# Probabilities times v in 64x64 quadrants, two units a visit, in a fused attention and feed-forward kernel

## The chip, the cores and the metric

The kernel runs on one core of a Trainium2 chip, in one launch. The metric is the device time of a run in microseconds (us), from the first to the last instruction with what lies around them. Times of the kernel before: 998.48, 1001.32 and 998.5 us, median 998.5. The engines are named as in the profile: PE does matrix products (PEld is its weight load, which overlaps them), DVE and ACT work on whole tiles and are the two that this kernel lets read PE's results, POOL scales tiles, and SP issues transfers.

## The reference, cut to what matters

Causal attention with a window of 128 positions and a slope per head, then a two-layer network on its output:

```
batch, heads, seq, dim = 8, 8, 576, 64
scores = q @ k.T / 8 + slope[h] * -(i - j)      where 0 <= i - j < 128, else -1e9
attn   = softmax(scores)
x      = (attn @ v), heads side by side         -> 4608 x 512
h      = x @ w_in                               512 x 2048
g      = h * erf(softplus(h))
out    = g @ w_out                              2048 x 512
```

All of it is float32.

## The kernel before

**Units.** The 4608 rows are cut into 12 chunks of 384. A unit is one chunk for two heads, so there are 48 units, four to a chunk, and `u // 4` is the chunk. Two chunks of three (32 units) are the first and second row blocks of a batch entry; every third chunk (`last`, 16 units) gathers the last 192 rows of two entries. `Attention.unit` plans one unit: it loads q, k and v (`load`), makes the scores of both heads in 64x64 tiles of PE (`scores`, line 478), adds the bias on DVE (505), exponentiates on ACT (515), sums and inverts on DVE (528, 529), scales on POOL (538), transposes on PE (557) into PSUM tiles `t`, copies those into `pT` (DVE or ACT, 417 and 415), and multiplies `pT` by v on PE (590) into a PSUM tile `px`. `px` is then copied as the high part of x (417 or 415) and subtracted from (600) to give the low part: fp32 numbers are split in two so that the network's products run in three quick passes.

**v times probabilities.** Here v lies in memory as 128 rows (64 positions of head 0, 64 of head 1) by 128 columns, in which head 0's rows hold zeros in head 1's columns and the other way round. One product of a 64-position block thus does both heads at once with a 128x128 weight, half of it zeros. A unit has six such products (four 192 columns wide, one 128, one 64), a unit of the last kind ten (two of 192, four of 128, four of 64). Each product is two records in the profile.

**Three stages.** Attention and the network's first pass run together: 6 of the 16 slices of the network's inner dimension, for each chunk as soon as its x is there (`h` line 797, `o` line 860). Meanwhile DVE and ACT bring the weights into two parts and park them in memory (lines 632 to 691). When all attention and all weight work is done, its memory is given back (`close`), the parked weights are fetched (720), and the second pass does the other ten slices (lines 999 and 1070).

**What sets the order.** `Plan.run` is a list scheduler that runs before the kernel is built. Every operation has a cost by engine, a due time `at` and the buffers that it takes; the plan goes through time, gives each engine the ready operation of lowest `at`, and writes each engine's instructions in that order, for good. Where an operation may go to DVE or ACT, the plan chooses. Buffers come from rings: PSUM tiles `s`, `t` and `px` share one ring `a` of three banks, v's ring has `NQ` buffers, `pT`'s has `TB`.

Of the kernel before, what the change touches and what calls it, by code (L numbers as in the profile page):

```python
# [8 lines left out]
F32 = mybir.dt.float32  # L9
# [8 lines left out]
B, H, S, D = 8, 8, 576, 64  # L18
NPAIR = H // 2
P = 128  # L20
# [3 lines left out]
NK = DM // P  # L24
NF = FF // P
CH = 384
# [11 lines left out]
WARM = 30  # L38

MB, KH, KS = 17, 3, 3  # L40
NQ, NKB, PB, XB, OB, TB = 2, 4, 9, 5, 5, 2

TE, NE = 4, 6
TA = 6.5
LL, LN, LT = 26, 0, 0
SQ = 0.36
LEAD = 45

# [10 lines left out]
TS, VL, NQF, SLP = 9, 8, 4, True  # L59
WB, PIE = "o1", 2  # L60
VE = -17
# [7 lines left out]
SUB = ALU.subtract  # L69
# [268 lines left out]
def fp32_us(n):  # L338
    return 2 * max(n / 1200.0 + 0.003, 0.111)


def dve(n, fast=False):
    return 0.047 + n * (0.00054 if fast else 0.00108)


def act(n, aps=0, src=0.088):
    return src + 0.093 * aps + n * 0.00084


def dma(nbytes, n=1, run=1536, eng="SP", out=False):  # L350
    packet = 9 + 0.0367 * run
    return dict(costs={eng: n * 0.42}, moved=nbytes / run * packet / 16e3 + 0.05 * n * (run > 2048), packet=packet, after=0.9 if out else 1.8 if run > 2048 else 1.3, count=n)


def unit_time(u):
    return TE * min(u, NE) + TA * max(0, u - NE) + UNITS.get(u, 0)
# [13 lines left out]
class Attention:  # L370


    def __init__(self, tc, plan, ctx, actx, qk, v, bias, ident, moe):
        self.nc, self.plan = tc.nc, plan
        self.qk, self.v = qk, v
        self.ident, self.moe = ident, moe
        nc, op = self.nc, plan.op
        sb = lambda name: actx.enter_context(tc.tile_pool(name=name, bufs=1))
        biases = sb("biases")
        self.bias = []  # L380
        rel = Buf(shape=[P, 4, D], ap=biases.tile([P, 4, D], F32, name="rel"))
        op(emit=lambda e: nc.scalar.dma_start(rel.all, bias), w=[rel], at=-40, **dma(P * 4 * D * 4, run=1024, eng="Act"))
        for g in range(NPAIR):
            b = Buf(shape=[P, 2, 4, D], ap=biases.tile([P, 2, 4, D], F32, name=f"bias{g}"))

            def slopes(e, b=b, g=g):
                for j in range(2):
                    slope = 2.0 ** (2 - 2 * g - j)
                    if e == "Act":
                        nc.scalar.mul(b[:, j], rel.all, slope)  # L390
                    else:
                        nc.gpsimd.tensor_scalar(b[:, j], rel.all, slope, 1.0, op0=ALU.mult, op1=ALU.mult)

            op({"Pool": 2 * (0.24 + 4 * D * 0.00086)} if SLP and g else {"Act": 2 * act(4 * D)}, slopes, r=[rel], w=[b], at=unit_time(g) - LL + 6)
            self.bias.append(b)
        self.ps_of = {}
        self.kp, self.pp, self.ptp, self.vp = (sb(n) for n in ("kp", "pp", "ptp", "vp"))
        self.ps = ctx.enter_context(tc.tile_pool(name="ps_a", bufs=1, space=PSUM))
        self.warm_up()
        for u in range(4 * moe.nch):  # L400
            self.unit(u)

    def warm_up(self):

# [14 lines left out]
    def load(self, u):  # L419


        c, g = u // 4, u % 4
        nc, op = self.nc, self.plan.op
        at = unit_time(u) - LL
        last = c % 3 == 2
        n, m = (640, 10) if last else (448, 6)
        i = c // 3 if last else c - c // 3
        src, vsrc = self.qk[last][i, g], self.v[last][i, g]
        qk = Buf(self.kp, [P, CH + 640], F32, "qk", NKB, f"qk{u}")
        v = Buf(self.vp, [P, 10, 2, D], F32, "v", NQ, f"v{u}")  # L430
        rows = lambda j: slice(j * D, (j + 1) * D)
        q = lambda t, j, h: qk[rows(j), t * P + h * D : t * P + (h + 1) * D]
        k = lambda j, x, w: qk[rows(j), CH + x : CH + x + w]
        if u:
            parts = [[qk]] * 3
            op(emit=lambda e: nc.sync.dma_start(qk[:, : CH + n], src), w=[qk], at=u - 29 if u < NQF else at, **dma(P * (CH + n) * 4, run=(CH + n) * 4))
        else:
            pieces = [Part(qk, i) for i in range((4, 2, 1)[PIE])]
            for i, (eng, issue, lo, hi) in enumerate(((
                    ("SP", nc.sync, 0, P), ("Act", nc.scalar, CH, CH + 192), ("Act", nc.scalar, CH + 192, CH + n), ("SP", nc.sync, P, CH)),  # L440
                    (("SP", nc.sync, 0, CH), ("SP", nc.sync, CH, CH + n)), (("SP", nc.sync, 0, CH + n),))[PIE]):
                op(emit=lambda e, issue=issue, lo=lo, hi=hi: issue.dma_start(qk[:, lo:hi], src[:, lo:hi]), w=[pieces[i]], at=-40 + i,
                   **dma(P * (hi - lo) * 4, run=(hi - lo) * 4, eng=eng))
            parts = [pieces[:2], pieces, pieces]
        op(emit=lambda e: nc.sync.dma_start(v[:, :m].rearrange("p x j d -> p (x j d)"), vsrc), w=[v], at=VE + 2 * u if u < NQF else at + VL,
           **dma(P * m * 2 * D * 4, run=m * 2 * D * 4))
        return parts, q, k, v

    def scores(self, u, ts, q, k, loaded, early, pts):
# [32 lines left out]
    def unit(self, u):  # L482


        nc, op = self.nc, self.plan.op
# [54 lines left out]

                op({"Pool": 2 * (0.24 + (3 - c0) * D * 0.00086)}, scaled, r=[p[t], sums[t]], w=[p[t]], at=at)

        at += LT
        px_at = at
        pT = Buf(self.ptp, [P, 8 * 192], F32, "pT", TB, f"pT{u}")
        run = lambda x, n, w: pT[:, x : x + n * w].rearrange("p (l c) -> p l c", c=w)
        parts = []
        for t in range(3):
            c0 = 0 if last or t else 1
# [11 lines left out]

            op({"PE": 0.109 * (3 - c0) + 0.005}, transposes, r=[p[t]], w=[ps], at=at)
            w = (3 - c0) * D
            step, x = (192, t * 384) if not last else ((192, 0), (192, 576), (576, 384))[t]
            part = Part(pT, slice(None), t)
            parts.append(part)

            def out(e, ps=ps, w=w, step=step, x=x):
                two = ps[:, : 2 * 192].rearrange("p (l c) -> p l c", c=192)
                self.copy(e, run(x, 2, step)[:, :, :w], two[:, :, :w])  # L570

            op({"DVE": dve(2 * w), "Act": act(2 * w, src=0.053)}, out, r=[ps], w=[part], at=at)

        px = Buf(self.ps, [P, 512], F32, "a", 3, f"px{u}", keep=0)
        if last:
            todo = [[(3 * s, kk, 5 * s + kk) for s in range(2) for kk in (2, 0, 1, 3, 4)]]
        else:
            todo = [[(0, 2, 0)], [(x, 2, x) for x in (3, 1, 2, 4, 5)]]
        for n, group in enumerate(todo):
            terms = []  # L580
            for base, kk, blk in group:
                if last:
                    i0, i1 = max(0, kk - 2), min(2, kk)
                    terms.append((blk, (base + i0) * 192 + (2 - kk + i0) * D, i1 - i0 + 1, (base + i0) * D))
                else:
                    terms.append((blk, base * 192, min(3, 6 - base), base * D))

            def products(e, terms=terms, first=n == 0, end=n + 1 == len(todo)):
                for x, (blk, src, m, to) in enumerate(terms):
                    nc.tensor.matmul(  # L590
                        px[:, to : to + m * D], lhsT=v[:, blk].rearrange("p j d -> p (j d)"), rhs=run(src, m, 256)[:, :, :D],
                        start=first and x == 0, stop=end and x + 1 == len(terms))

            op({"PE": sum(fp32_us(m * D) for _, _, m, _ in terms) + 0.005}, products,
               r=[v, *(parts if n or last else parts[:2])], w=[px], at=at + 0.1)

        hi, lo = self.moe.x_parts[c][g]
        op({"DVE": dve(CH), "Act": act(CH, src=0.053)},
           lambda e: self.copy(e, hi.all, px[:, :CH]), r=[px], w=[hi], at=at + 0.1)
        op({"DVE": dve(CH)}, lambda e: nc.vector.tensor_tensor(lo.all, px[:, :CH], hi.all, SUB),  # L600
           r=[px, hi], w=[lo], at=at + 0.1)
        if g % 2:
            self.moe.save_x(c, g // 2, at + 0.1)


class Weights:
# [560 lines left out]
def _layout(q, k, v, moe_w_in, moe_w_out):  # L1167
# [7 lines left out]
    qk_a = flat(np.concatenate([qT[..., :CH], gap, kT[..., :CH]], 4))  # L1175
    both = lambda a, lo, hi: [a[s::2, ..., lo:hi] for s in range(2)]
    qk_c = flat(np.concatenate([*both(qT, CH, 512), *both(qT, 512, S), *both(kT, 256, S)], 4))
    vs = np.zeros((nb, NPAIR, 2, D, S // D, 2, D), np.float32)
    for b in range(nb):
        for j in range(2):  # L1180
            vs[b, :, j, :, :, j] = v[b, j::2].reshape(NPAIR, S // D, D, D).transpose(0, 2, 1, 3)
    v_a = np.ascontiguousarray(vs[..., :6, :, :]).reshape(nb, NPAIR, P, 768)
    v_c = np.concatenate([vs[s::2, ..., 4:, :, :].reshape(nb // 2, NPAIR, P, 640) for s in range(2)], 3)
    bits = lambda a: a.view(np.int64)
    wi = np.ascontiguousarray(bits(moe_w_in).reshape(NK, P, NF, P).transpose(2, 1, 0, 3))
    wo = np.ascontiguousarray(bits(moe_w_out))
    row = (np.arange(P) % 64)[:, None]
    rel = WIN + row - np.arange(192)[None, :]
# [25 lines left out]
```

## Time and profile before

| what | value |
|---|---|
| runs | 998.48, 1001.32, 998.5 us |
| span of the profiled execution | 996.5 us |
| median less span | 2.0 us |
| busy in the span | PE 983.5, PEld 873.2, DVE 682.7, ACT 668.9, POOL 155.0 us |
| DMA | 172.17 MB, mean 173 GB/s |

The page gives the span of one profiled execution; the 2.0 us by which the median is above it are what lies before the first and after the last instruction. A line such as L590 is line 590 of the kernel. PE's busy time counts a matmul from its start to its modelled end; since matmuls overlap, the durations of single records sum to more than the time that a group takes. What a group takes is read in the chain of waits, whose pieces do not overlap.

### The profile page before, as it was taken

The page shows a single profiled execution, that of the slowest core. Times are in us where ns is not written, and L with a number is a line of the kernel's source. Part 1 is how long each engine was busy: PE and PEld are TensorE (multiplying, and loading weights), DVE is VectorE, ACT ScalarE, POOL GpSimd, SP SyncE. Part 2 cuts the span into 40 slices and gives each one's busy share as a digit, 9 for nine tenths or more (in the row PEclk, how much of TensorE's full clock was granted, in tenths as well). Part 3 has the DMA queues.
Part 4 walks back from the last instruction along what each step waited for, and adds up shares of the span by engine and source line. Part 5 has one row for each costly group of instructions (what it writes and reads, how often), then busy time and mean ns, then how long its engine had stood idle before and what let it go on. Part 6 is the DMA issues. An engine that isn't in the chain of part 4 may idle for free.

```text
span 996.5 us, 17094 instructions
## 1 busy us (share of the span) xinstructions
PE 983.5 (99%) x6168; PEld 873.2 (88%) x6168; DVE 682.7 (69%) x1627; ACT 668.9 (67%) x1261; POOL 155.0 (16%) x300
## 2 busy tenths in 40 slices
PE   9899999999999999999999999999999999999998
PEld 7788898888888888889999899898998989989896
DVE  6999899789998987465557367367457547544433
ACT  6898788888878878667866464545555464464652
POOL 4613433223314432131000000000000000000000
PEclk9999999999999999999999999999999999999999
DMA  9754685678875675554974243152242341420302
GB/s 366 268 168 146 223 269 172 255 269 300 283 265 174 236 258 183 175 191 156 373 259 148 86 183 116 44 190 75 85 161 80 109 159 43 147 96 2 125 1 74
DMA packets 63076, 172.17 MB, mean 173 GB/s; under 512 B 7056, under 2 KB 7184, under 8 KB 62992
## 3 DMA queue, kind: packets, MB, share of 16 engines
q1 hardware_dynamic: 62848, 170.95, 49.5%
q8 instruction: 49, 0.80, 0.4%
q14 instruction: 35, 0.29, 0.1%
q10 hardware_dynamic: 144, 0.13, 0.0%
HBM read 118.88 MB, written 52.17 MB: 172 GB/s over the span
## 4 chain that ended last, share of the span: by engine, by line
PE 89%; DVE 7%; ACT 2%; issue 1%; POOL 1%; DMA 1%; SPq 0%; DVEq 0%; POOLq 0%
PE o L860 14%; PE h L797 13%; PE pa L999 13%; PE po L1070 12%; PE pa L1070 12%; PE px L590 8%; PE pc L999 6%; PE s L478 4%; PE t L557 4%; PE pb L999 3%; DVE p L505 1%; ACT p L515 1%; POOL p L538 1%; PE warm_ps L410 1%; DVE wti L637 0%
## 5 line engine op out<-in xcount | busy, mean ns | idle before, releaser
L538 POOL TENSOR_SCALAR p<-p,st 128x192 f32<-128x192 f32 (+1 forms) x288 | 152.0, 550 | 293.1 <-DVE st L529 175.6
L797 PE MATMUL h<-x,wi 128*128 128x384 f32 x864 | 174.3, 344 | 0.0
L780 ACT COPY hs<-pa 128x384 f32<-128x384 f32 x92 | 44.3, 481 | 180.1 <-PE pa L999 179.5
L797 PEld LDWEIGHTS h<-x,wi 128*128 128x128 f32 x864 | 149.2, 188 | 7.9 <-issue 4.2
L860 PE MATMUL o<-wo,gh 128*128 128x512 f32 x432 | 141.6, 408 | 0.0
L515 ACT ACTIVATE p<-p,st 128x192 f32<-128x192 f32 (+1 forms) x288 | 123.9, 433 | 16.3 <-DVE st L505 16.2
L999 PE MATMUL pa<-t,p 128*128 128x384 f32 x540 | 108.9, 336 | 0.0
L590 PEld LDWEIGHTS px<-pT,v 128*128 128x128 f32 x704 | 100.7, 191 | 5.8 <-DVE x L600 2.0
L590 PE MATMUL px<-pT,v 128*128 128x192 f32 (+2 forms) x704 | 102.4, 296 | 1.7 <-DVE x L600 1.7
L999 PEld LDWEIGHTS pa<-t,p 128*128 128x128 f32 x540 | 96.4, 188 | 5.9
L1070 PE MATMUL po<-ho,gh 128*128 128x512 f32 x270 | 91.0, 391 | 0.0
L1070 PE MATMUL pa<-ho,gh 128*128 128x512 f32 x270 | 90.5, 389 | 0.0
L782 DVE COPY hs<-pa 128x384 f32<-128x384 f32 x28 | 15.6, 557 | 108.4 <-PE pa L999 108.4
L860 PEld LDWEIGHTS o<-wo,gh 128*128 128x128 f32 x432 | 75.1, 189 | 13.6 <-issue 4.7
L860 PE MATMUL o<-wo,gl 128*128 128x512 f32 x216 | 85.3, 395 | 0.0
L505 DVE CUSTOM_DVE_ANT_0 p<-s,bias 128x192 f32<-128x192 f32 x224 | 66.2, 350 | 8.0 <-PE s L478 7.7
L1070 PE MATMUL po<-ho,gl 128*128 128x512 f32 x180 | 71.3, 396 | 0.0
L1050 DVE TENSOR_TENSOR hs<-s,hs 128x768 f32<-128x768 f32 x60 | 56.2, 951 | 20.9 <-ACT s L1042 20.9
L1070 PE MATMUL pa<-ho,gl 128*128 128x512 f32 x180 | 70.1, 389 | 0.0
L1010 DVE TENSOR_TENSOR hs<-pc,hs 128x384 f32<-128x384 f32 x60 | 33.3, 556 | 52.0 <-PE pc L999 37.7
L557 PE MATMUL t<-ident,p 128*128 128x128 f32 x400 | 62.1, 275 | 4.0 <-POOL p L538 2.5
L557 PEld LDWEIGHTS t<-ident,p 128*128 128x128 f32 x400 | 48.0, 143 | 15.2 <-POOL p L538 6.8
(259 smaller groups left out, 1858.8 us busy)
## 6 DMA issues: line engine op xcount, KB each, us to landing
xd<-x SPq DMA_DIRECT2D x24, 768.0 KB, 6.0
qk<-qk_a SPq DMA_DIRECT2D x32, 416.0 KB, 4.8
v<-v_a SPq DMA_DIRECT2D x32, 384.0 KB, 3.8
v<-v_c SPq DMA_DIRECT2D x16, 640.0 KB, 4.1
pd<-ot SPq DMA_DIRECT2D x36, 256.0 KB, 3.3
out<-pd SPq DMA_DIRECT2D x36, 256.0 KB, 4.0
p<-wd SPq DMA_DIRECT2D x35, 256.0 KB, 5.3
wri<-w_in SPq DMA_DIRECT2D x16, 512.0 KB, 7.2
```

Source lines behind the costliest of these rows:

```text
L478: nc.tensor.matmul(bank[h * D : (h + 1) * D, x : x + n], lhsT=q(t, j, h), rhs=k(j, off[h], n), start=True, stop=True)
L505: nc.vector.tensor_tensor_reduce(out=pt[:, c0:, j, :], in0=ps[j][0][:, ps[j][1] : ps[j][1] + n].rearrange("p (c d) -> p c d", d=D), in1=se ...
L515: nc.scalar.activation(dst, dst, AF.Exp, bias=low[t][:, j : j + 1], scale=-1.0, accum_out=sums[t][:, j : j + 1])
L538: nc.gpsimd.tensor_scalar(dst, dst, sums[t][:, j : j + 1], 1.0, op0=ALU.mult, op1=ALU.mult)
L557: nc.tensor.matmul(two[:, :, (2 - cb) * D : (3 - cb) * D], lhsT=p[t][:, cb].rearrange("p j d -> p (j d)"), rhs=self.ident[:, :], is_transp ...
L590: nc.tensor.matmul(px[:, to : to + m * D], lhsT=v[:, blk].rearrange("p j d -> p (j d)"), rhs=run(src, m, 256)[:, :, :D], start=first and x ...
L780: self.nc.scalar.copy(out, src)
L797: nc.tensor.matmul(ps[:, :CH], lhsT=ww[:, cs], rhs=xx[:, k], start=(k2 + k + n == 0), stop=(k2 + k + n == 4),)
L860: nc.tensor.matmul(po.all, lhsT=g[:, j, cs], rhs=w.all, start=(u["start"] and n == 0), stop=(u["end"] and n == 2),)
L999: nc.tensor.matmul(dst[:, :CH], lhsT=wv[i](k), rhs=xb[l][:, k], start=start and k + n == 0, stop=k + n == 3, skip_group_check=not start)
L1050: op({"DVE": dve(2 * CH)}, lambda e, s=s, hs=hs: V.tensor_tensor(hs.all, s.all, hs.all, ALU.mult), r=[s, *parts], w=parts, at=at, port=True)
L1070: nc.tensor.matmul(po.all, lhsT=g[:, k, cs], rhs=w.all, start=start and n == 0, stop=end and n == 2)
```

## The change

Scores are already made in 64x64 tiles; now v times probabilities is too. v comes without zeros (`v` is 128 rows by 64 columns a block, half the bytes), and the two units of a pair are multiplied in one visit of PE (`pair`), after both are transposed. A block's four products are head 0 and 1 of the first unit and head 1 and 0 of the second, one for each quadrant of the array: rows by the head, since that is where v and `pT` lie, columns by the head for the first unit and swapped for the second. Products from the upper 64 rows all go to PSUM bank `px[0]`, those from the lower ones to `px[1]`. So `px[0]` holds heads 0 and 2 of the four, `px[1]` heads 3 and 1, and the rows of w_in are put into that order before the launch. `pT` keeps its data in another layout (18 blocks of 64), its ring has 3 buffers in place of 2, v's has 4 in place of 2. Copies and subtractions of `px` are as many and as large as before.

```diff
--- before.py
+++ after.py
-NQ, NKB, PB, XB, OB, TB = 2, 4, 9, 5, 5, 2
+NQ, NKB, PB, XB, OB, TB = 4, 4, 9, 5, 5, 3
...
-LL, LN, LT = 26, 0, 0
+LL, LN, LT, PXL = 26, 0, 0, 0.1
...
-        for u in range(4 * moe.nch):
-            self.unit(u)
+        for u in range(0, 4 * moe.nch, 2):
+            self.pair(u, [self.unit(u), self.unit(u + 1)])
...
-        v = Buf(self.vp, [P, 10, 2, D], F32, "v", NQ, f"v{u}")
+        v = Buf(self.vp, [P, 10, D], F32, "v", NQ, f"v{u}")
...
-        pT = Buf(self.ptp, [P, 8 * 192], F32, "pT", TB, f"pT{u}")
-        run = lambda x, n, w: pT[:, x : x + n * w].rearrange("p (l c) -> p l c", c=w)
+        pT = Buf(self.ptp, [P, 18, D], F32, "pT", TB, f"pT{u}")
...
-            step, x = (192, t * 384) if not last else ((192, 0), (192, 576), (576, 384))[t]
+            ys = slice(2 * t, 2 * t + 2) if not last else (slice(0, 2), slice(3, 5), slice(2, 6, 3))[t]
...
-                self.copy(e, run(x, 2, step)[:, :, :w], two[:, :, :w])
+                every = pT[:, :].rearrange("p (y b) d -> p y (b d)", b=3)
+                self.copy(e, every[:, ys, :w], two[:, :, :w])
...
-        px = Buf(self.ps, [P, 512], F32, "a", 3, f"px{u}", keep=0)
-        if last:
...
-            def products(e, terms=terms, first=n == 0, end=n + 1 == len(todo)):
-                for x, (blk, src, m, to) in enumerate(terms):
-                    nc.tensor.matmul(
-                        px[:, to : to + m * D], lhsT=v[:, blk].rearrange("p j d -> p (j d)"), rhs=run(src, m, 256)[:, :, :D],
-                        start=first and x == 0, stop=end and x + 1 == len(terms))
-
-            op({"PE": sum(fp32_us(m * D) for _, _, m, _ in terms) + 0.005}, products,
-               r=[v, *(parts if n or last else parts[:2])], w=[px], at=at + 0.1)
...
+        return v, pT, parts
+
+    def pair(self, u, units):
+
+        nc, op = self.nc, self.plan.op
+        c, g = u // 4, u % 4
+        last = c % 3 == 2
+        at = unit_time(u + 1) + LN + LT + PXL
+        px = [Buf(self.ps, [P, 512], F32, "a", 3, f"px{u + j}", keep=0) for j in range(2)]
+        terms = []
+        for s, kk in [(s, kk) for s in range(2) for kk in (2, 0, 1, 3, 4)] if last else [(0, kk) for kk in (0, 3, 1, 2, 4, 5)]:
+            if last:
+                i0, i1 = max(0, kk - 2), min(2, kk)
+                first = 3 * s + i0
+                terms.append((5 * s + kk, 3 * first + 2 - kk + i0, i1 - i0 + 1, first * D))
+            else:
+                terms.append((kk, 3 * kk, min(3, 6 - kk), kk * D))
+
+        def products(e):
+            for x, (blk, src, m, to) in enumerate(terms):
+                for swap, (v, pT, _) in enumerate(units):
+                    for j in (swap, 1 - swap):
+                        rows, cols = slice(j * D, (j + 1) * D), slice((j ^ swap) * D, ((j ^ swap) + 1) * D)
+                        nc.tensor.matmul(
+                            px[j][cols, to : to + m * D], lhsT=v[rows, blk, :], rhs=pT[rows, src : src + 4 * m - 3 : 4, :],
+                            start=x == 0, stop=x + 1 == len(terms))
+
+        op({"PE": SQ + sum(2 * max(m * D / 1200 + 0.002, 0.06) for _, _, m, _ in terms)}, products,
+           r=[b for v, _, parts in units for b in (v, *parts)], w=px, at=at)
+        for j in range(2):
+            hi, lo = self.moe.x_parts[c][g + j]
+            op({"DVE": dve(CH), "Act": act(CH, src=0.053)},
+               lambda e, hi=hi, j=j: self.copy(e, hi.all, px[j][:, :CH]), r=[px[j]], w=[hi], at=at)
+            op({"DVE": dve(CH)}, lambda e, hi=hi, lo=lo, j=j: nc.vector.tensor_tensor(lo.all, px[j][:, :CH], hi.all, SUB),
+               r=[px[j], hi], w=[lo], at=at)
+        self.moe.save_x(c, g // 2, at)
...
-    vs = np.zeros((nb, NPAIR, 2, D, S // D, 2, D), np.float32)
-    for b in range(nb):
-        for j in range(2):
-            vs[b, :, j, :, :, j] = v[b, j::2].reshape(NPAIR, S // D, D, D).transpose(0, 2, 1, 3)
-    v_a = np.ascontiguousarray(vs[..., :6, :, :]).reshape(nb, NPAIR, P, 768)
-    v_c = np.concatenate([vs[s::2, ..., 4:, :, :].reshape(nb // 2, NPAIR, P, 640) for s in range(2)], 3)
+    vs = np.ascontiguousarray(v.reshape(nb, NPAIR, 2, S // D, D, D).transpose(0, 1, 2, 4, 3, 5)).reshape(nb, NPAIR, P, S // D, D)
+    v_a = np.ascontiguousarray(vs[..., :6, :]).reshape(nb, NPAIR, P, 384)
+    v_c = np.concatenate([vs[s::2, ..., 4:, :].reshape(nb // 2, NPAIR, P, 320) for s in range(2)], 3)
     bits = lambda a: a.view(np.int64)
-    wi = np.ascontiguousarray(bits(moe_w_in).reshape(NK, P, NF, P).transpose(2, 1, 0, 3))
+    heads = [h + 4 * k2 for k2 in range(NPAIR // 2) for h in (0, 2, 3, 1)]
+    wi = bits(moe_w_in).reshape(H, D, NF, P)[heads].reshape(NK, P, NF, P)
+    wi = np.ascontiguousarray(wi.transpose(2, 1, 0, 3))
```

The order of instructions moves with it. In PE's order, the visits of units 26 and 27 stood like this before (px is the product, t a transpose, o and h products of the first pass; a number behind a name is that of the unit or slice):

```order
L590 MATMUL px26_3391<-pT26_3330,v26_3140 128x192 x4
L590 MATMUL px26_3391<-pT26_3330,v26_3140 128x128
L590 MATMUL px26_3391<-pT26_3330,v26_3140 128x64
L557 MATMUL t27_0_3404<-ident_62,p27_0_3280 128x2x64 x2
L557 MATMUL t27_1_3409<-ident_62,p27_1_3284 128x2x64 x3
L860 MATMUL o0_24_3415<-wo0_1033,gh24_2956 128x512 x2
L860 MATMUL o0_24_3415<-wo0_1033,gl24_2975 128x512
L860 MATMUL o1_24_3425<-wo0_1033,gh24_2956 128x512 x2
L860 MATMUL o1_24_3425<-wo0_1033,gl24_2975 128x512
L557 MATMUL t27_2_3435<-ident_62,p27_2_3294 128x2x64 x3
L590 MATMUL px27_3441<-pT27_3419,v27_3202 128x192
```

and stand like this now, as the first ten of 24 rows of one visit (line 590 is now 595, 557 is 554):

```order
L864 MATMUL o1_24_3578<-wo0_1123,gh24_3206 128x512 x2
L864 MATMUL o1_24_3578<-wo0_1123,gl24_3210 128x512
L595 MATMUL px26_3585<-pT26_3461,v26_3218 64x192
L595 MATMUL px27_3587<-pT26_3461,v26_3218 64x192
L595 MATMUL px27_3587<-pT27_3525,v27_3225 64x192
L595 MATMUL px26_3585<-pT27_3525,v27_3225 64x192
L595 MATMUL px26_3585<-pT26_3461,v26_3218 64x192
L595 MATMUL px27_3587<-pT26_3461,v26_3218 64x192
L595 MATMUL px27_3587<-pT27_3525,v27_3225 64x192
L595 MATMUL px26_3585<-pT27_3525,v27_3225 64x192
```

Unit 26's products stood alone ahead of unit 27's transposes; now all of the pair's stand in one run behind the transposes of both.

At the end of attention on PE, unit 47's product and what follows it, before:

```order
L797 MATMUL h59_5824<-x9_0_4647,wi5_959 128x384 x6
L797 MATMUL h59_5824<-x9_1_4984,wi5_959 128x384 x6
L590 MATMUL px47_5845<-pT47_5803,v47_5684 128x192
L590 MATMUL px47_5845<-pT47_5803,v47_5684 128x64
L590 MATMUL px47_5845<-pT47_5803,v47_5684 128x128 x2
L590 MATMUL px47_5845<-pT47_5803,v47_5684 128x64
L590 MATMUL px47_5845<-pT47_5803,v47_5684 128x192
L590 MATMUL px47_5845<-pT47_5803,v47_5684 128x64
L590 MATMUL px47_5845<-pT47_5803,v47_5684 128x128 x2
L590 MATMUL px47_5845<-pT47_5803,v47_5684 128x64
L860 MATMUL o0_48_5455<-wo5_1448,gh52_5491 128x512 x2
L860 MATMUL o0_48_5455<-wo5_1448,gl52_5513 128x512
```

and now, the end of the visit of units 46 and 47:

```order
L595 MATMUL px46_6091<-pT46_6008,v46_5665 64x64
L595 MATMUL px47_6093<-pT46_6008,v46_5665 64x64
L595 MATMUL px47_6093<-pT47_6071,v47_5669 64x64
L595 MATMUL px46_6091<-pT47_6071,v47_5669 64x64
L801 MATMUL h57_6081<-x9_1_5240,wi3_900 128x384 x6
L864 MATMUL o0_48_5812<-wo3_1423,gh50_5724 128x512 x2
L864 MATMUL o0_48_5812<-wo3_1423,gl50_5757 128x512
L864 MATMUL o0_48_5812<-wo4_1542,gh52_5869 128x512 x2
L864 MATMUL o0_48_5812<-wo4_1542,gl52_5914 128x512
```

The visit now stands ahead of the second half of slice-unit h57 and of h58 and h59, which were done by then before. Counted to the end of the first pass, 144 h and 171 o products stood behind the last px, now 174 and 189.

On DVE, the end of the last weight's preparation (wto15) stood beside the copies of unit 40's transposes before:

```order
L640 SCALAR_TENSOR_TENSOR wqo15_4801<-wro15_4535,wqo15_4801 128x512
L645 TENSOR_TENSOR wto15_4855<-wto15_4855,wqo15_4801 128x512
L417 COPY pT40_4955<-t40_0_4945 128x2x128
L683 CAST wh__4960<-wto15_4855 128x512
L686 TENSOR_TENSOR wto15_4855<-wto15_4855,wh__4960 128x512
L417 COPY pT40_4955<-t40_1_4963 128x384
L417 CAST x9_1_4984<-px39_4915 128x384
```

and stands ahead of the copies of units 44 and 45 (`x11_0`) now:

```order
L649 TENSOR_TENSOR wto15_5748<-wto15_5748,wqo15_5714 128x512
L687 CAST wh__6021<-wto15_5748 128x512
L690 TENSOR_TENSOR wto15_5748<-wto15_5748,wh__6021 128x512
L417 CAST x11_0_6038<-px44_5958 128x384
L417 CAST x11_0_6038<-px45_5960 128x384
L605 TENSOR_TENSOR x11_0_6038<-px44_5958,x11_0_6038 128x384
L605 TENSOR_TENSOR x11_0_6038<-px45_5960,x11_0_6038 128x384
L417 COPY pT46_6008<-t46_1_6025 128x384
```

The weight work on DVE now ends some five units later in attention. In the whole order 15 copies of `t` into `pT` have moved from ACT to DVE (77 were on DVE, 92 are).

## Rows read from the trace of the kernel before

**Rows 1.** The page's first part: busy us, share of the span, instructions.

```profile
PE 983.5 (99%) x6168; PEld 873.2 (88%) x6168; DVE 682.7 (69%) x1627; ACT 668.9 (67%) x1261; POOL 155.0 (16%) x300
```

**Rows 2.** Busy time by stretch: stretch, length, engines' busy us, granted clock, DMA share, GB/s.

```profile
0.00:25.00 25.00, 22.55 (x252) 19.77 (x252) 15.86 (x74) 16.69 (x61) 11.32 (x31) 1.00 0.95 366
25.00:120.00 95.00, 90.27 (x672) 77.78 (x673) 93.04 (x280) 83.55 (x200) 40.24 (x66) 1.00 0.56 195
120.00:200.00 80.00, 79.76 (x620) 70.86 (x619) 69.75 (x213) 67.20 (x155) 24.96 (x49) 1.00 0.70 238
200.00:400.00 200.00, 199.34 (x1558) 172.99 (x1556) 174.56 (x554) 163.30 (x398) 65.50 (x129) 1.00 0.72 246
400.00:461.50 61.50, 61.06 (x429) 53.57 (x428) 34.99 (x97) 45.55 (x91) 13.01 (x28) 1.00 0.40 140
461.50:511.50 50.00, 50.00 (x253) 45.29 (x252) 25.68 (x35) 36.08 (x39) 0.00 (x0) 1.00 0.87 306
511.50:996.50 485.00, 480.54 (x2395) 432.92 (x2393) 268.84 (x380) 256.51 (x321) 0.00 (x0) 1.00 0.32 108
```

**Rows 3.** The page's chain that ended last, by line.

```profile
PE o L860 14%; PE h L797 13%; PE pa L999 13%; PE po L1070 12%; PE pa L1070 12%; PE px L590 8%; PE pc L999 6%; PE s L478 4%; PE t L557 4%; PE pb L999 3%; DVE p L505 1%; ACT p L515 1%; POOL p L538 1%; PE warm_ps L410 1%; DVE wti L637 0%
```

**Rows 4.** Timeline of PE at the end of attention and first pass.

```profile
456.72 2.54 PE L590 MATMUL px<-pT,v 128*128 128x192 f32 x20
459.07 0.71 PE L860 MATMUL o<-wo,gh 128*128 128x512 f32 x2
...
511.47 1.23 PE L999 MATMUL pa<-11_0_6185,p 128*128 128x384 f32 x6
```

**Rows 5.** The chain of waits, 213 to 262 us: start, length, what.

```profile
224.63 2.38 PE px L590 x20
...
227.35 0.33 PE px L590 x2
227.68 1.39 PE o L860 x6
...
233.42 1.69 PE px L590 x12
...
238.44 1.05 PE h L797 x6
239.48 1.03 PE s L478 x24
240.51 1.27 PE h L797 x6
```

**Rows 6.** Transfers of v: count, KB each, us to landing.

```profile
v<-v_a SPq DMA_DIRECT2D x32, 384.0 KB, 3.8
v<-v_c SPq DMA_DIRECT2D x16, 640.0 KB, 4.1
```

**Rows 7.** DVE by line, 0 to 461.5 us: busy, mean ns, idle before.

```profile
L417 DVE COPY pT<-t 128x384 f32<-128x384 f32 (+1 forms) x77 | 38.7, 511 | 8.5 <-PE t L557 8.3
L844 DVE TENSOR_TENSOR gl<-hs,gh 128x768 fp32r<-128x768 f32 x29 | 27.7, 956 | 0.2
...
L600 DVE TENSOR_TENSOR x<-px,x 128x384 fp32r<-128x384 f32 x48 | 26.0, 547 | 4.1 <-ACT x L415 3.9
...
L417 DVE CAST x<-px 128x384 fp32r<-128x384 f32 x26 | 14.3, 551 | 25.5 <-PE h L797 14.2 <-PE px L590 11.3
```

**Rows 8.** PE's waits: for whom, us in total, times, longest.

```profile
PE t L557 <- POOL p L538: 2.5, 5, 1.3
PE px L590 <- DVE x L600: 1.7, 1, 1.7
PE warm_ps L410 <- DVE warm L408: 1.1, 1, 1.1
```

More of the change, by code (lines that the diff above doesn't have):

```diff
@@ L444, in load @@
             parts = [pieces[:2], pieces, pieces]
-        op(emit=lambda e: nc.sync.dma_start(v[:, :m].rearrange("p x j d -> p (x j d)"), vsrc), w=[v], at=VE + 2 * u if u < NQF else at + VL,
-           **dma(P * m * 2 * D * 4, run=m * 2 * D * 4))
+        op(emit=lambda e: nc.sync.dma_start(v[:, :m].rearrange("p x d -> p (x d)"), vsrc), w=[v], at=VE + 2 * u if u < NQF else at + VL,
+           **dma(P * m * D * 4, run=m * D * 4))
         return parts, q, k, v
@@ L541, in unit @@
                 op({"Pool": 2 * (0.24 + (3 - c0) * D * 0.00086)}, scaled, r=[p[t], sums[t]], w=[p[t]], at=at)
-        at += LT
-        px_at = at
-        pT = Buf(self.ptp, [P, 8 * 192], F32, "pT", TB, f"pT{u}")
-        run = lambda x, n, w: pT[:, x : x + n * w].rearrange("p (l c) -> p l c", c=w)
+        pT = Buf(self.ptp, [P, 18, D], F32, "pT", TB, f"pT{u}")
         parts = []
@@ L563, in unit, with out @@
             w = (3 - c0) * D
-            step, x = (192, t * 384) if not last else ((192, 0), (192, 576), (576, 384))[t]
+            ys = slice(2 * t, 2 * t + 2) if not last else (slice(0, 2), slice(3, 5), slice(2, 6, 3))[t]
             part = Part(pT, slice(None), t)
             parts.append(part)
-            def out(e, ps=ps, w=w, step=step, x=x):
+            def out(e, ps=ps, w=w, ys=ys):
                 two = ps[:, : 2 * 192].rearrange("p (l c) -> p l c", c=192)
-                self.copy(e, run(x, 2, step)[:, :, :w], two[:, :, :w])
+                every = pT[:, :].rearrange("p (y b) d -> p y (b d)", b=3)
+                self.copy(e, every[:, ys, :w], two[:, :, :w])
@@ L572, in unit @@
             op({"DVE": dve(2 * w), "Act": act(2 * w, src=0.053)}, out, r=[ps], w=[part], at=at)
-        px = Buf(self.ps, [P, 512], F32, "a", 3, f"px{u}", keep=0)
-        if last:
[L576 to L586, printed above, removed]
-            def products(e, terms=terms, first=n == 0, end=n + 1 == len(todo)):
-                for x, (blk, src, m, to) in enumerate(terms):
-                    nc.tensor.matmul(
-                        px[:, to : to + m * D], lhsT=v[:, blk].rearrange("p j d -> p (j d)"), rhs=run(src, m, 256)[:, :, :D],
-                        start=first and x == 0, stop=end and x + 1 == len(terms))
-            op({"PE": sum(fp32_us(m * D) for _, _, m, _ in terms) + 0.005}, products,
-               r=[v, *(parts if n or last else parts[:2])], w=[px], at=at + 0.1)
@@ L597, in unit @@
[L597 to L603, printed above, removed]
+        return v, pT, parts
[30 more added lines that the diff above has]
+        self.moe.save_x(c, g // 2, at)
```

## The prediction

> **What bounds the kernel now.** I read the page's busy times first, then the stretches, the chain of waits, and the waits of PE and DVE. PE is busy 983.5 of 996.5 us and no other engine over 69% [rows 1], and nearly all of the chain that ended last is PE's, 8% of it v times probabilities, L590 [rows 3]. So work taken from PE comes off the end, as long as PE isn't made to wait instead. The share of a whole span hides where that could happen; the stretches show it. From 25 to 120 us DVE is busy 93.04 of 95 us; from 200 to 400 us it is 174.56 of 200, 87%; from 511.5 on, 268.84 of 485 [rows 2]. Attention's last px starts at 456.72 us and ends by 459.07, and the second pass starts at 511.47 [rows 4]. Between these PE does first-pass work alone, while the weights come in at 306 GB/s [rows 2]. What follows 511.47 is the same before and after the change and waits for PE only. The question is thus how much earlier attention ends.
>
> **What v times probabilities costs now.** In the chain a unit's px is 1.69 us (12 records), a last unit's 2.38 (20 records), and one 192-wide product 0.33 (2 records) [rows 5]. 32 units of 1.69 and 16 of 2.38 are 54.1 + 38.1 = 92.2 us of PE.
>
> **What it costs then.** No row shows v times probabilities in 64x64 tiles, but the scores are made so: 12 products a unit, three to a quadrant, of 128, 192 and 192 columns, 512 columns by each quadrant. The group takes 1.03 us in the chain, and the h group behind it 1.27 in place of 1.05 [rows 5], so 1.25 in all. At the full array's rate of 0.33 us for 192 columns, 512 columns are 0.88. So the four quadrants run side by side at the full rate, and the change of tile size costs the other 0.37; run two at a time they would take at least 1.76.
>
> A visit of an ordinary pair has 4 x 192 + 128 + 64 = 960 columns for each quadrant, 5 x 0.33 + 0.37 = 2.02 us; of a last pair 1152, 6 x 0.33 + 0.37 = 2.35. 16 x 2.02 + 8 x 2.35 = 51.1 us. In PE's new order no visit stands next to a scores group, so each pays its own 0.37. PE is relieved of 92.2 - 51.1 = **41.1 us**.
>
> Bounds. The narrow products are what no row prices in quadrants. At full width they cost more than their columns: of a last unit's 2.38 us, 0.66 are the two wide ones, so eight narrow ones take 0.215 each, where 64 columns alone would be 0.11. If a 64-wide one kept about 0.2 in quadrants, 48 of them (one in each ordinary visit, four in each last) would add 4.3 us. If all the scores' 1.25 went by columns, a visit would be 2.34 or 2.81 and the saving 92.2 - 59.9 = 32.3. Nothing here makes it larger than 41.1. I take 41.1, since the wide products carry most columns and the scores' rate was seen for them.
>
> **What moves.** The new order leaves 174 h and 189 o products behind the last px, where 144 and 171 stood. At 1.05 us for six h and 1.39 for six o [rows 5] that is 30 x 0.175 + 18 x 0.232 = 9.4 us of PE work moved behind attention. It costs nothing in the sum, and it lets attention end earlier still: with nothing waiting, at 459.1 - 41.1 - 9.4 = 408.6 us. It also lengthens the 52 us in which the weights' fetch is hidden, so the fetch is no new wait.
>
> **What DVE makes of it.** The copies of px and its subtractions stay 48 and 48 at some 0.55 us [rows 7]. Up to attention's end DVE is busy 15.86 + 93.04 + 69.75 + 174.56 + 34.99 = 388.2 us [rows 2]. In the new order 15 copies of t move from ACT to DVE, 15 x 0.511 = 7.7 us [rows 7], and one pair of first-pass slices moves behind attention, two tiles of 768 columns at 0.956 and copies, some 3 us as an estimate: 393 us. With the 9.1 us that DVE cannot use at the start (25 less 15.86), DVE alone would need 402, beside PE's 408.6. Two engines that are both nearly full, in an order fixed ahead, make each other wait, so some of the 41.1 is lost. I price that in two stretches.
>
> Before 120 us: twelve units, eight ordinary and four last, 8 x 1.69 + 4 x 2.38 = 23.0 us before and 4 x 2.02 + 2 x 2.35 = 12.8 after, 10.2 saved on PE. But there DVE was at 97.9%. PE's matmul busy share of that stretch is 95%, its weight loads' 77.78 of 95, 82%; from 461.5 to 511.5, where PE has only its own work, they are 45.29 of 50, 91% [rows 2]. So PE has slack there already. I count half as lost, 5.1, between 0 and 10.2. The Trainium skill, Trainium Kernel Development and Optimization, section Best Practices, says to judge by the weight loads' busy share and not the matmuls'. By the matmuls' 95% that stretch would be PE's and all 10.2 would count (a sum of 41.1); by the loads' 82% it is DVE's and none would (30.9); the trace's DVE row sides with the second.
>
> From 120 us on: DVE has 393 - 108.9 = 284 us to do. With the first loss alone attention would end at 408.6 + 5.1 = 413.7, and that stretch begins 5.1 earlier, so it has 413.7 - 114.9 = 298.8 us: DVE at 95%, between the 87% and the 97.9% seen. I take 4 us of waiting, an estimate between 0 (97.9% was held for 95 us) and 17 (DVE at 90%: 284 / 0.90 = 315.6).
>
> The rest at nothing: v's transfers fall from 32 x 384 + 16 x 640 KB to half [rows 6]. DMA is 95% busy only in the first 25 us; four units' v there are 0.77 MB less, 2.1 us at 366 GB/s [rows 2], and the start waits for q and k and for DVE more than for v: 0 taken, 2.1 the most. The order of w_in's rows and the wider rings cost no instruction.
>
> **Sum.** 41.1 - 5.1 - 4 = 32.0 us. The profiled span of 996.5 becomes 964.5; the median stands 2.0 above the span, so 998.5 becomes **966.5 us**.
>
> **Rivals.**
> 1. *PE's whole saving arrives.* DVE keeps up at 96% and over, as it did at 97.9%: 998.5 - 41.1 = 957.4, with v's transfers 955.3. For it: PE's largest waits of before sum to 2.5, 1.7 and 1.1 us [rows 8], though DVE was full for 95 us. Against it: there DVE's fullness cost PE slack that no wait row shows.
> 2. *DVE sets the pace.* None of the first 10.2 and 17 us of waiting later: 41.1 - 10.2 - 17 = 13.9 saved, 984.6. For it: 393 us of DVE in some 410. The Trainium skill, TensorEngine Tiling (Array Packing), section PSUM Bottleneck, says that tiling speeds PE but not the emptying of PSUM, which may become the bound. Here rows 7 have that emptying; the trace of before agrees only for 25 to 120 us.
> 3. *The banks are the bound, and it gets slower.* A visit takes two of ring a's three banks at once, and they come free after two copies and two subtractions, 4 x 0.55 = 2.2 us [rows 7]. In the new order a transpose, which wants a bank of that ring, stands right behind 16 of the 24 visits. If PE stood still for 2.2 us at each visit, 24 x 2.2 = 52.8 against 41.1: 998.5 + 11.7 = 1010. It decides from 41.1 / 24 = 1.7 us a visit. Against it: the third bank, h and o products in between, and one such wait of 1.7 us in the whole trace [rows 8].
> 4. *The quadrants don't overlap as the scores' do*, because these accumulate and stand in another quadrant order; two at a time, a visit is 0.37 + 10 x 0.33 = 3.67 or 0.37 + 12 x 0.33 = 4.33, together 93.4: 998.5 + 1.2, no change. Against it: same tiles, same banks by rows.
>
> **How the numbers follow.** Forecast 0.52 (958 to 976, its own range, from both losses' bounds), rival 1 0.15, rival 2 0.22, rival 3 0.06, rival 4 0.05. The range is 953 to 985: the low end is rival 1 with v's transfers and a little off, the high end rival 2, which a dear narrow product would reach too (4.3 more on 966.5 with half its losses again); rivals 3 and 4 stay out. Faster by over 0.3% (3 us, about what a measurement here tells from none) 0.89, within it 0.05, slower 0.06.
>
> **What would show it.** The px records become 1408 of 64x64; a visit is near 2.0 and 2.35 us in the chain, scores and transposes as before. Attention's last px ends near 418 us, and the second pass starts near 479. DVE is some 95% busy from 115 us to there; PE waits some 10 us for DVE and ACT, at L595 or the transposes. Wrong would be a visit of 2.5 us or more (price), a px end near 409 (rival 1) or past 430 (rival 2), and long waits of the transposes for the copies of px (rival 3). The second pass should be the same 485 us; if it isn't, the sum rests on a wrong part.

## The result, and the profile after

The changed kernel takes 963.37 us (963.07 to 963.68, 4 runs) against 998.79 us of the kernel before; the ratio is 0.9644, 95% interval 0.963 to 0.9657. It is 35.4 us faster; 966.5 was forecast, 32.0 faster. The span fell from 996.5 to 961.6 us. One of the four runs of the full-width pairs below took 1391.51 us at a granted clock of 0.655; their time is given as the median of the other three, 1004.95 us (1005.25 with it). Page of the kernel after, first part, against [rows 1]:

```profile
PE 942.8 (98%) x6872; PEld 820.6 (85%) x6872; DVE 685.5 (71%) x1641; ACT 662.2 (69%) x1247; POOL 160.0 (17%) x300
```

PE's busy time is 40.7 us less, DVE's and ACT's within 7 us of what they were: the relief is PE's. The chain of waits after, 200 to 262 us, columns as in [rows 5], shows what a visit takes:

```profile
206.80 0.33 PE t L554 x3
207.12 0.70 PE o L864 x3
207.82 2.15 PE px L595 x80
209.97 0.48 PE t L554 x3
...
235.65 1.79 PE px L595 x48
237.44 0.91 PE o L864 x3
...
257.87 1.79 PE px L595 x48
259.67 0.48 PE t L554 x3
```

The piece behind a visit is longer than elsewhere (0.48 for three transposes in place of 0.33, 0.91 for three o in place of 0.70); I read that as the return to full-width tiles. So an ordinary visit is 1.79 + 0.21 = 2.00 us and a last one 2.15 + 0.15 = 2.30; forecast were 2.02 and 2.35. 16 x 2.00 + 8 x 2.30 = 50.4 us, and PE is relieved of 92.2 - 50.4 = 41.8 us. By the visit at 257.87 us an ordinary one would be 1.94, so the 41.8 hold to some 1 us. The timeline of PE at the end of attention and of the first pass, against [rows 4]:

```profile
412.09 2.22 PE L595 MATMUL px<-pT,v 64*64 64x192 f32 x80
414.24 1.34 PE L801 MATMUL h<-x,wi 128*128 128x384 f32 x6
...
476.04 1.23 PE L1003 MATMUL pa<-11_0_6492,p 128*128 128x384 f32 x6
```

Attention ends at 414.2 us (forecast near 418), and 61.8 us of first-pass work follow where 52.4 did: the 9.4 that moved. The second pass starts 35.4 us earlier and, in the last row of the stretches, is as long as before (485 us, [rows 2]):

```profile
0.00:25.00 25.00, 21.37 (x278) 17.33 (x278) 16.73 (x81) 16.84 (x62) 12.60 (x34) 1.00 0.93 356
25.00:75.00 50.00, 42.47 (x421) 34.80 (x421) 49.08 (x157) 44.41 (x115) 19.37 (x35) 0.93 0.53 192
...
75.00:400.00 325.00, 322.32 (x3253) 266.86 (x3252) 304.36 (x957) 284.55 (x678) 119.86 (x220) 1.00 0.62 214
...
200.00:400.00 200.00, 199.06 (x1989) 165.83 (x1989) 185.66 (x589) 174.28 (x413) 70.07 (x136) 1.00 0.64 223
...
476.00:961.50 485.50, 480.61 (x2395) 432.95 (x2394) 268.51 (x380) 256.53 (x321) 0.00 (x0) 1.00 0.31 108
```

Two of these stretches in the kernel before (its others are in [rows 2]):

```profile
25.00:75.00 50.00, 45.71 (x349) 40.50 (x349) 49.83 (x157) 45.34 (x115) 20.80 (x36) 1.00 0.60 217
75.00:400.00 325.00, 323.66 (x2502) 281.14 (x2500) 287.52 (x889) 268.71 (x637) 109.90 (x207) 1.00 0.68 234
```

Here stands the question for the experiments: 41.8 us were taken from PE and 35.4 arrived. Most of the missing 6.4 us are early: from 75 to 400 us PE is idle for 2.7 us against 1.3, in the first 25 us for 3.6 against 2.5, and from 25 to 75 us for 7.5 against 4.3. The granted clock of that last stretch is 0.93: between its two levels, 2.4 and 1.2 GHz, that is some 7 us of the 50 at the lower one, 3.5 us of work. It is doubtful that these 3.5 us reach the end: of the kernel's four runs the two with a mean granted clock of 0.996 took 963.07 and 963.49 us, the two with 0.998 took 963.25 and 963.68.

### The profile page after: what moved, and what is told of

Same layout as the page of the kernel before. It is cut to its first block, busy times and chain, and to the rows that moved or that the text cites. A ratio compares the mean times of both kernels' runs of the same rounds, so it can differ in the third digit from the quotient of the medians.

```text
span 961.6 us, 18491 instructions
## 1 busy us (share of the span) xinstructions
PE 942.8 (98%) x6872; PEld 820.6 (85%) x6872; DVE 685.5 (71%) x1641; ACT 662.2 (69%) x1247; POOL 160.0 (17%) x300
## 4 chain that ended last, share of the span: by engine, by line
PE 86%; DVE 9%; DMA 2%; ACT 2%; issue 1%; POOL 0%; DVEq 0%; ACTq 0%; POOLq 0%
PE o L864 13%; PE pa L1003 13%; PE h L801 13%; PE po L1074 13%; PE pa L1074 12%; PE pc L1003 7%; PE s L478 4%; PE px L595 4%; PE t L554 4%; PE pb L1003 3%; DVE p L505 2%; ACT p L515 1%; DVE pT L417 1%; DVE gl L848 1%; PE warm_ps L410 1%
## 5 line engine op out<-in xcount | busy, mean ns | idle before, releaser
L538 POOL TENSOR_SCALAR p<-p,st 128x192 f32<-128x192 f32 (+1 forms) x288 | 157.0, 564 | 243.3 <-DVE st L529 171.9
L801 PEld LDWEIGHTS h<-x,wi 128*128 128x128 f32 x864 | 151.6, 190 | 9.3 <-issue 3.1
L554 PE MATMUL t<-ident,p 128*128 128x128 f32 x400 | 64.5, 280 | 7.8 <-POOL p L538 5.0
L478 PE MATMUL s<-qk 64*64 64x192 f32 (+1 forms) x1152 | 58.9, 323 | 4.2 <-issue 1.7
L1074 PEld LDWEIGHTS pa<-ho,gh 128*128 128x128 f32 x270 | 50.7, 188 | 10.9
```

Source lines behind the costliest of these rows:

```text
L478: nc.tensor.matmul(bank[h * D : (h + 1) * D, x : x + n], lhsT=q(t, j, h), rhs=k(j, off[h], n), start=True, stop=True)
L538: nc.gpsimd.tensor_scalar(dst, dst, sums[t][:, j : j + 1], 1.0, op0=ALU.mult, op1=ALU.mult)
L554: nc.tensor.matmul(two[:, :, (2 - cb) * D : (3 - cb) * D], lhsT=p[t][:, cb].rearrange("p j d -> p (j d)"), rhs=self.ident[:, :], is_transp ...
L801: nc.tensor.matmul(ps[:, :CH], lhsT=ww[:, cs], rhs=xx[:, k], start=(k2 + k + n == 0), stop=(k2 + k + n == 4),)
L1074: nc.tensor.matmul(po.all, lhsT=g[:, k, cs], rhs=w.all, start=start and n == 0, stop=end and n == 2)
```

## The experiments

**Pairs without quadrants.** v with its zeros, 128x128 weights, w_in in its plain order, v's ring at 2 (twice the width leaves no room for 4), the rest as changed:

```diff
-                for swap, (v, pT, _) in enumerate(units):
-                    for j in (swap, 1 - swap):
...
+                for i, (v, pT, _) in enumerate(units):
+                    nc.tensor.matmul(
+                        px[i][:, to : to + m * D], lhsT=v[:, blk].rearrange("p j d -> p (j d)"), rhs=pT[:, src : src + 4 * m - 3 : 4, :],
```

> Pairs stay, quadrants go: one visit for two units, but with 128x128 weights half of zeros as in the kernel before (v twice as wide, its ring 2 buffers, w_in's rows in their plain order). Theory (the whole gain is PE's, from quadrants): PE does 92.2 us of px again and pays no change of tile size, so the time is back at 995 to 1003, and a visit in the chain is 2 x 1.69 or 2 x 2.38 us. Rival (the pairing, pT's third buffer and the order bring part of it): under 985.

Measured 1004.95 us, ratio to the kernel before 1.0057 (1.004 to 1.0074): a little outside the theory's range, and slower than the kernel before. Chain and stretch of it:

```profile
202.48 4.82 PE px L593 x40
```

```profile
25.00:75.00 50.00, 44.55 (x336) 38.41 (x337) 49.62 (x159) 42.11 (x103) 20.73 (x35) 0.93 0.59 217
```

A visit is 4.82 us for two last units, twice 2.38 and a little. From here to the changed kernel are 41.6 us, as much as the visits above are cheaper (41.8) within the noise: the quadrants, with the order that the plan makes for them, give the whole gain. What is missing is what the rest of the change costs, 1004.95 - 998.52 = 6.4 us. With it come the same 0.93 of clock, and 5.5 us of idling (4.3 before), from 25 to 75 us.

**The same without pairs.** Each unit's full-width px on its own, pT's new layout and third buffer kept:

```diff
-        for u in range(0, 4 * moe.nch, 2):
-            self.pair(u, [self.unit(u), self.unit(u + 1)])
+        for u in range(4 * moe.nch):
+            self.single(u, self.unit(u))
```

> The full-width pairs (1005.3 us) with the pairing undone: each unit's px on its own when its transposes are copied, as in the kernel before, but with pT's new layout and its third buffer. Theory (pairing by itself costs some 6 us, all of it PE idle from 25 to 75 us, and layout and ring cost nothing): 997 to 1000. Rival (the layout of pT or its ring makes the full-width pairs slow): 1003 or more.

Measured 1001.54 us, ratio 1.0029 (1.0019 to 1.0038): between the two. Pairing alone is 1004.95 - 1001.54 = 3.4 us, with some 2 us of play by the two intervals. The other 2.8 us came with layout and ring and the order that the plan made with them, in which PE idles later:

```profile
25.00:75.00 50.00, 46.27 (x362) 40.19 (x363) 49.79 (x166) 46.04 (x122) 20.86 (x36) 1.00 0.63 228
75.00:400.00 325.00, 320.75 (x2469) 279.02 (x2468) 282.86 (x869) 266.84 (x629) 107.55 (x203) 1.00 0.66 230
```

From 25 to 75 us it idles 3.7 us at full clock, less than the kernel before: the early loss belongs to the pairs. From 75 to 400 us it idles 4.3 us, where the paired kernels idle 2.3 (full width) and 2.7, so the two parts do not simply add.

**v's ring.** `NQ` 2 in place of 4 in the changed kernel.

> The changed kernel with 2 buffers of v in place of 4, as the full-width pairs had. Theory: v is loaded long before its visit, so the plan moves a little and the time stays at 962 to 966; the 42 us between the full-width pairs and the changed kernel are then the quadrants' own. Rival (the ring of 4 is what the pair needs): 969 or more.

Measured 963.94 us (2 runs, 962.78 and 965.1), 0.6 us above the changed kernel and within the noise: the ring of 4 does not explain the 41.6 us.

**v's bytes.** Every transfer of v issued twice.

> The changed kernel with every transfer of v issued twice into the same buffer, so v's bytes are again those of the kernel before and v comes later. Theory (v's bytes are worth nothing, the first 25 us wait for q, k and DVE): 962 to 965. Rival (the halved transfers brought 2 us or more at the start): 965.5 or more.

Measured 962.94 us (0.9648, 0.9629 to 0.9666): the halved transfers brought nothing that can be measured here, to some 2 us either way. The second issue also changes the plan's order. The start is later all the same:

```profile
0.00:25.00 25.00, 19.24 (x228) 15.88 (x228) 16.17 (x73) 17.03 (x62) 13.02 (x32) 1.00 0.94 358
```

PE is busy for 2.1 us less there than in the changed kernel, and the end is no later.

**Two quadrants at a time.** Same order of everything else; inside a visit the loops change places, so that all of the first unit's products go ahead of the second's:

```diff
-            for x, (blk, src, m, to) in enumerate(terms):
-                for swap, (v, pT, _) in enumerate(units):
+            for swap, (v, pT, _) in enumerate(units):
+                for x, (blk, src, m, to) in enumerate(terms):
```

> The changed kernel with the same products, the same order of everything else, but inside a visit all of the first unit's products before the second's. Theory (quadrants overlap with their neighbours in the issue order, and there are then only two different ones): a visit is 0.37 + 10 x 0.33 = 3.67 us, a last one 4.33, together 42 us more on PE: 998 to 1006. Rival (PE finds free quadrants further down its queue): a visit stays near 2.0 and the time at 963.

Measured 994.15 us (0.9949, 0.9934 to 0.9965). Chain:

```profile
219.82 3.85 PE px L595 x76
223.68 0.48 PE t L554 x3
...
237.56 3.14 PE px L595 x44
...
250.46 3.14 PE px L595 x44
253.61 0.89 PE o L864 x3
```

Visits are 3.14 and 3.85 us where the changed kernel has 1.79 and 2.15; 16 x 1.35 + 8 x 1.70 = 35.2 us more, of which 30.8 show in the time. (PE idles 17.6 us in the whole span, 1.2 less than in the changed kernel, and its clock is 1.00 from 25 to 75 us, not 0.93.) I had said 3.67 and 4.33. With the longer piece behind, as above, they are 3.3 and 4.0: the price of the columns alone, 10 and 12 x 0.33, with nothing left of the 0.37 for the change of tile size. In the changed kernel the visits do take 0.35 more than their columns (2.00 for 1.65). So it is not shown that this 0.35 is the change of tile size; a part may be that four quadrants overlap less than fully, and no run tells the two apart. The theory holds, its price was high: most of the gain hangs on an order in which neighbouring products name all four quadrants and not two.

**DVE relieved.** In both kernels, order kept to the row, four of the five steps that bring the first pass's 12 weight slices into one word work on 64 of 512 columns only and leave the others out:

```diff
-                t.all, q.all, -(1 << 31), t.all, op0=ALU.bitwise_and, op1=ALU.bitwise_or)),
+                t[:, :n], q[:, :n], -(1 << 31), t[:, :n], op0=ALU.bitwise_and, op1=ALU.bitwise_or)),
...
+        t = self.plain(which, f, at, Buf(pool, [P, DM, 2], I32, tag, 1, "wr" + nm), W1R, 64)
```

> The kernel before, in the very same order, but four of the five DVE steps that bring each of the first pass's 12 weight slices into one fp32 word work on 64 columns in place of 512 (the rest of the weights stays rough): some 22 us of DVE less before 100 us, nothing else. Theory (PE waits on DVE there): 3 to 5 us faster than the kernel before, 994 to 996. Rival (DVE's fullness costs nothing): 998 to 999.

> The changed kernel, in its very same order, with the same four narrow DVE steps for the 12 first weight slices. Theory (the gap between the 41 us that PE is relieved of and the 35.4 that arrived is PE waiting on DVE in the first 75 to 100 us): 7 to 11 us faster than the changed kernel, 952 to 956, so that the difference to the kernel before with the same narrow steps is 40 to 42 us. Rival (the gap lies in the visits: banks held, copies bunched): it gains no more than the kernel before does, difference still 35 to 36.

Measured 994.34 and 958.24 us (0.9948 and 0.9591 of the kernel before). Each kernel gains some 4 to 5 us, and the difference is 36.1, not 40 to 42: the theory that DVE alone holds back the changed kernel fell. The kernel before with this cut, and the changed one:

```profile
25.00:75.00 50.00, 48.78 (x385) 43.41 (x384) 41.51 (x155) 47.51 (x115) 17.46 (x38) 1.00 0.64 232
```

```profile
25.00:75.00 50.00, 43.08 (x446) 36.13 (x446) 42.62 (x171) 47.62 (x128) 21.11 (x43) 1.00 0.55 199
```

DVE is down to 83 and 85%, but ACT is up at 95% in both, and PE idles 1.2 and 6.9 us.

**DVE and ACT relieved.** Beside that cut, the first 12 slice-units have copies in place of softplus and erf, without the table loads:

```diff
+            if pairs[0][0][0]["U"] < 12:
+                for us, n, n2, hs, s, at in pairs:
+                    A.copy(s[:, :n], hs[:, :n])
+                    A.copy(s[:, :n], s[:, :n])
+                return
```

> The kernel before, same order, with the narrow DVE steps and, beside them, the first pass's first 12 slice-units with softplus and erf as plain copies on ACT and none of their table loads (their g is not the reference's): some 22 us of DVE and 25 to 30 us of ACT less in the first 120 us. With both engines relieved PE is the bound from the start on: 3 to 6 us below the kernel with narrow steps alone (994.3), 988 to 992.

> The same two cuts in the changed kernel, same order. Theory now (in the first 75 us PE waits on the softmax chain, which DVE and ACT pace together, so that relieving DVE alone only hands the bound to ACT): the difference to the kernel before with both cuts rises from 36.1 to 39 to 42 us. Rival (px of a pair comes later because it waits for both units, whatever DVE and ACT do): the difference stays at 35 to 37.

Measured 993.29 and 954.98 us (0.995 and 0.9561). The kernel before gains 1 us more, less than I said; the changed one 3.3. The difference is 38.3 us, just under the theory's 39 to 42 and above the rival's 35 to 37. The runs of these two kernels spread over 1.4 and 1.1 us, so this favours the theory, and a part of the rival's may remain. Their stretches:

```profile
25.00:75.00 50.00, 48.80 (x385) 43.32 (x383) 41.09 (x153) 35.18 (x106) 17.88 (x37) 1.00 0.63 230
```

```profile
25.00:75.00 50.00, 45.75 (x530) 38.38 (x528) 43.58 (x170) 37.90 (x120) 21.08 (x44) 1.00 0.54 197
```

PE idles 1.2 and 4.25 us. Set side by side with PE's idle time, from 25 to 75 us and in the whole span (the span less PE's busy time, from the pages), what is missing from 41.8:

| compared | arrived | missing | PE idle, 25 to 75 us | PE idle, whole span |
|---|---|---|---|---|
| before, changed | 35.4 | 6.4 | 4.3, 7.5: 3.2 more | 13.0, 18.8: 5.8 more |
| both with DVE relieved | 36.1 | 5.7 | 1.2, 6.9: 5.7 more | 10.0, 15.9: 5.9 more |
| both with DVE and ACT relieved | 38.3 | 3.5 | 1.2, 4.25: 3.05 more | 9.4, 13.1: 3.7 more |

What is missing goes with PE's idle time in the whole span, and most of that is early. In the first row the stretch from 25 to 75 us gives only 3.2 us of it; the 3.5 us of the lower clock, which this row alone has, would fill the gap, but its four runs make that doubtful. With runs of one kernel about 1 us apart, 6.4 and 5.7 cannot be told from each other; 3.5 is less.

**Another order.** Two tries at a faster version, changing due times alone, and then the plan's costs of DVE and ACT with due times fitted to them:

```diff
-    return 0.047 + n * (0.00054 if fast else 0.00108)
+    return 0.12 + n * (0.00048 if fast else 0.001)
...
-    return src + 0.093 * aps + n * 0.00084
+    return src + 0.07 + 0.093 * aps + n * 0.00084
```

> The changed kernel with other due times for the plan (units, first pass, weight preparation), no change to any instruction: the table of the kernel before was left as it was when px became cheaper. Theory: the first 75 us, where PE has too little work, give 2 to 4 us back: 959 to 961. Rival (the order is as good as DVE and ACT allow): 963 or more.

> The changed kernel with the plan's costs of DVE and ACT set to what the profile shows (a 384-column copy on DVE 0.50 us in place of 0.46, on ACT 0.45 in place of 0.38, a 768-column one on ACT 0.80 in place of 0.73) and due times fitted to these. No instruction changes, only order and the choice between DVE and ACT. Theory (the other due times alone, 966.0, failed because the plan thought DVE and ACT cheaper than they are, so that PE met late copies): 956 to 961, with less PE idle from 25 to 75 us than the changed kernel's 7.5. Rival (the order is not what costs the 6 us): 963 or more.

Measured 965.98 (0.9669, 0.9654 to 0.9683) and 963.58 us (0.9647, 0.9631 to 0.9663): neither is faster than the changed kernel, and the second still has PE idle for 7.0 us from 25 to 75. Both theories fell; within these two orders nothing of the 6 us comes back.

## Why the prediction was right, and where not

- **The price of a visit** was right: 2.00 and 2.30 us for 2.02 and 2.35. The scores' visits were the right row to price from, and the bounds from the narrow products were not needed: a last visit, with its eight narrow products a quadrant, took 0.30 us more than an ordinary one for 192 columns more, which are 0.33 us at the full array's rate. That its 0.37 is the change of tile size, as the prediction says, is not shown (two quadrants at a time).
- **What moves** was right to the tenth: 9.4 us of first pass behind attention, the weights' fetch still hidden (PE is busy for all 53 us from 423 to 476), the second pass unchanged.
- **Before 120 us**, "I count half as lost, 5.1": the size was near (up to 75 us PE idles 11.2 us against 6.7, 4.4 more), the reason only partly right. I named DVE. Relieving DVE alone changed the missing part by 0.7 us, which the noise could be, relieving ACT too by 2.9; the rest stays, and the full-width pairs show a loss of that size without any cheaper px. The chain of waits of the kernel after shows what stands behind a pair:

```profile
35.97 1.85 PE px L595 x48
37.82 0.40 DVE pT L417
38.22 0.47 DVE x L417
38.80 0.19 DVE st L529
38.99 0.45 DVE x L605
39.72 0.16 issue
39.88 2.85 POOL p L538 x3
42.78 0.55 PE t L554 x3
```

  From 37.82 to 42.78 us the chain runs over DVE and POOL: 0.92 us are px's copy and subtraction, 2.85 are POOL's scaling, which the next transposes wait for. PE itself stands idle for 1.5 of these 5 us, since it has transposes, scores and a group of the first pass to do. Its two longest idle times from 25 to 75 us are 1.73 us for POOL, before the transposes at 31.18, and this one:

```profile
57.52 1.74 PE L478 MATMUL s<-qk 64*64 64x192 f32 x24 [1.68 <-issue]
```

  For these 1.68 us the profile names no releaser. They end 0.1 us after the second subtraction of units 6 and 7 does (DVE, L605, two from 56.42 us on, 1.00 us together), and the scores are those of unit 8, the first last unit, which go into all three banks of ring `a`, while the pair's px holds two. So I read a wait for the pair's banks here. That the pair's copies come in one bunch and hold its banks is argued from these times; no run changed the bunch or the banks alone, so their share stays open.
- **From 120 us on**, "I take 4 us of waiting": mis-sized. PE idled 2.7 us from 75 to 400 us, 1.4 more than before, with DVE at 93% from 200 to 400. This loss, taken 2.6 us too high, and the visits, priced 0.7 us too dear, are most of the 3.4 us by which the kernel came out faster than forecast; the early loss was near by size and not by cause. The Trainium skill, TensorEngine Tiling (Array Packing), section PSUM Bottleneck, warns that the emptying of PSUM may become the bound; this trace does not bear it out from 200 to 400 us, where DVE is at 93% and PE idles 0.9 of 200 us.
- **The rivals.** 1 would have needed the early loss to vanish (957.4); 2 needed late waits that didn't come. 3, the banks: PE waits for the subtraction L605 for 0.7 and 0.5 us in all, and with the 1.7 us that the profile gives to nobody for some 2.9, far from 1.7 a visit; a part of the early loss may be this. 4 is refuted for this issue order, and the kernel with two quadrants at a time shows that it would have been near true for another (994.15).

PE's waits after, columns as in [rows 8]:

```profile
PE t L554 <- POOL p L538: 5.0, 9, 1.7
PE s L478 <- issue: 1.7, 1, 1.7
...
PE t L554 <- DVE x L605: 0.7, 1, 0.7
PE t L554 <- DVE pT L417: 0.6, 1, 0.6
PE s L478 <- DVE x L605: 0.5, 1, 0.5
```

## What to carry to other kernels

Price a new form of product from the nearest group that already has that form, with what that group takes beyond its columns, and then ask stretch by stretch whether the engine that is relieved has other work there: here the saving came through nearly whole from 75 us on, where the first pass could fill PE, and most of what was lost was lost before, where DVE (98% from 25 to 75 us) and ACT (89%) set the pace. All four quadrants overlapped only when neighbours in the issue order named all four (1.79 us a visit, 3.14 with two at a time), so the loop order inside the group is part of the gain. An experiment that keeps the order to the row and makes one engine's work smaller tells a bound from a coincidence; here it showed that the engine with the highest share was not the only bound.

## What the runs showed that was not expected

In the profiled runs the granted clock fell in the changed kernel's early stretch, and not in the kernel before's. The stretches of the kernel after:

```profile
25.00:40.00 15.00, 10.56 (x107) 8.24 (x106) 14.42 (x54) 11.97 (x46) 8.63 (x17) 0.89 0.89 344
...
55.00:60.00 5.00, 3.21 (x31) 1.79 (x29) 5.00 (x11) 4.94 (x6) 0.00 (x0) 0.87 0.41 134
60.00:65.00 5.00, 4.89 (x38) 3.92 (x38) 4.97 (x21) 4.77 (x16) 0.00 (x0) 0.79 0.23 85
```

A mean of 0.79 to 0.89 is a spell at 1.2 GHz beside one at 2.4. In the first row PE is busy for 10.56 of the 15 us, in the second for 3.21 of 5, after which the lower level lasts into the third, where PE is busy again (4.89 of 5). Over the 50 us that is the 3.5 us of PE's work reckoned above. But idling alone does not decide it: from 25 to 40 us the full-width pairs have PE busier than the kernel before, and their clock falls, its does not. The two rows, full-width pairs first:

```profile
25.00:40.00 15.00, 11.70 (x88) 8.96 (x89) 14.75 (x62) 11.12 (x43) 8.76 (x18) 0.81 0.84 333
```

```profile
25.00:40.00 15.00, 11.12 (x87) 9.44 (x88) 14.90 (x62) 12.99 (x48) 10.10 (x20) 1.00 0.98 381
```

In the changed kernel with DVE relieved PE idled 6.9 us from 25 to 75 us and the clock stayed at 1.00. What decides it stays open. And halving v's transfers, which looked like a gain by itself, was worth nothing measurable.
